# Leaving out nine idle TensorE matmuls of zeros at the start of a gated linear attention and feed-forward kernel

## Chip, cores and metric

The kernel runs on one core of a Trainium2 chip. The metric is the device time of one execution in microseconds (us); lower is better. The median of three timed executions is compared. A separate execution was recorded by the hardware profiler, and every trace row below is from it.

## What is computed

The inputs are q, k, v and alpha of shape (4, 8, 768, 48): batch, heads, sequence and head size. Per batch and head a 48x48 state runs along the sequence, and its output feeds a bilinear feed-forward layer.

```python
def _attn_ref(q, k, v, alpha):
    state = np.zeros((B, H, D, D), dtype=np.float32)
    for t in range(S):
        state = alpha[:, :, t, :, None] * state + np.einsum('bhd,bhe->bhde', k[:, :, t], v[:, :, t])
        y[:, :, t] = np.einsum('bhd,bhde->bhe', q[:, :, t], state)
    return y

x = attn_out.transpose(0, 2, 1, 3).reshape(B * S, H * D)      # 3072 x 384
a = x @ w_a                                                   # 384 x 1536
b = x @ w_b
out = (a * b) @ w_out                                         # 1536 x 384
```

## The kernel before, in words

The work is cut into six chunks. A chunk holds two batches (called `u` 0 and 1) and 256 positions of the sequence, two to a partition. For a chunk the kernel takes the logarithm of alpha, forms running sums of it along the sequence with a triangular matrix on TensorE, and takes exponentials of these sums to scale q and k. Then it transposes the scaled q and k on TensorE or by DMA, forms scores, masks them, multiplies by v and carries the state over to the next chunk. The result, already transposed, goes through the feed-forward layer in units of 128 hidden columns.

The order of all instructions is written by hand in a table of text, `PROGRAM`. Each line names a chunk and then short operations, and the kernel issues them in exactly that order; each engine then works through its own instructions in that order and waits on semaphores for what it needs. The part of the table around the change is the first stage, chunk 0, which has the following steps.

- `ld a`, `ld k`, `ld q` with `Y` (SP's queue) or `P` (POOL's queue) load the inputs; `0a` and `0b` are the two halves of the heads of batch 0, and `1` is all of batch 1. `c1` fills small constants on VectorE, among them `wz`, a 128x512 tile of zeros (L471).
- `ln` takes logarithms on ScalarE into the tile `la` (L554).
- `B` forms running sums, by four fp32 matmuls for one half of the heads (L589 and L590). In chunk 0 there are four such groups: `B 0b`, `B 0a`, `B 1a` and `B 1b`. The profile shows each fp32 matmul as two records, so each group has eight records.
- `E` takes the two exponentials of the sums on ScalarE (L665, into the tile shown as `prod`), and `mk` and `mq` scale k and q with them on VectorE into `QKp` (L676).
- `dk` forms the sums over 64 positions on TensorE by 32 small matmuls (L698), and `de` takes their exponentials on ScalarE into `bl` (L719).
- `C` transposes the eight head pairs of one half of the heads on TensorE, keys first and then queries (L736), and `Ce` copies the result out of PSUM into `kqT` on VectorE (L960).
- `v` and `vs` copy v into its place on ScalarE (L769 and L958).
- `D` forms scores (L837), `K` the new state (L792), `k` scales it into `Sm` (L819), `SB` multiplies the carried state by the queries (L866), `M` masks (L846), `Y` multiplies by v (L866).
- `a` and `b` are the units of the feed-forward layer (L921), `o` its second product (L943).

Two places of the first stage hold an operation `fill n i`: it issues n matmuls of zeros by zeros into PSUM bank i, whose result nothing reads.

```python
    def fill(n, i):
        for _ in range(n):
            nc.tensor.matmul(bank(i), lhsT=wz[:, :C], rhs=wz, start=True, stop=True)

    def cum_both(ch, uh, i):                                   # "B"
        ...
        for r in range(2):
            nc.tensor.matmul(p[:, r], lhsT=ut, rhs=x[:, :, 0, :], start=True, stop=False)
            nc.tensor.matmul(p[:, r], lhsT=ut if r else uts, rhs=x[:, :, 1, :], start=False, stop=True)
```

The seven matmuls of `fill 7 0` are TensorE's first instructions. The two of `fill 2 0` stand between the two groups of transposes of batch 0.

Of the kernel before, what the change touches and what calls it, by code (L numbers as in the profile page):

```python
# [14 lines left out]


PROGRAM = """
0: cm 0; c1; cz 0 b P; ci; ld a 0b Y; c1a; ld a 0a Y; ln 0b; cu; cz 1 b P; fill 7 0; cu2 V
0: cz 0 q V; cus; ld k 0b Y; ld k 0a Y; B 0b 2; ld q 0b Y; ln 0a; B 0a 0; ld v 0 P; ld q 0a Y; ld a 1 P; cs 0 m P
0: E 0b i; mk 0b V; ld k 1 P; ld q 1 P; cm 1; W b 0 256; cz 0 v P; E 0b b; mq 0b V; ld v 1 P; W a 256 768; dk 0 2  # L20
0: C 0 1 3; E 0a i; mk 0a V; cz 1 q P; E 0a b; mq 0a V; v 0 S; Ce 0 1 V; fill 2 0; W a 0 256; de 0; W b 256 512
0: C 0 0 1; Ce 0 0 V; D 0 1 2; K 0 0 0; vs 0 0 S; W b 512 768; cs 1 m P
1: ld a 0 P
0: D 0 0 4; k 0 0 V; SB 0 0; M 0 0; ln 1; B 1a 6
# [1153 lines left out]
```

## Time and profile before

| what | value |
|---|---|
| median of three timed executions | 189.08 us (189.05 to 189.28) |
| time of the profiled execution | 190.44 us |
| its span, first to last instruction | 188.7 us |
| TensorE (PE) busy | 181.9 us, 96% of the span |
| VectorE (DVE) busy | 152.6 us, 81% |
| ScalarE (ACT) busy | 120.1 us, 64% |
| GpSimd (POOL) busy | 53.6 us, 28% |
| mean granted TensorE clock | 0.991 of full speed |

The profiled execution is 1.74 us longer than its span, the part before the first and after the last instruction. PE is the matmul side of TensorE and PEld its weight loads. Times of rows are counted from the start of the span. In a row of the timeline stand the start, the length of the merged instructions, engine, source line, operation, output and inputs, shape, the count, and in brackets the idle time of the engine just before with what released it. Matmuls are pipelined and the records of neighbours overlap, so a busy PE is not one at its peak. In a row of a table by stretches, the fields are the length of the stretch, each engine's busy time with its count of instructions, the granted TensorE clock (PEclk), the busy share of DMA and its GB/s.

### The profile page before, as it was taken

The numbers are of one execution on the slowest core, as the hardware profiler recorded it, in microseconds if no ns is written. First come the engines' busy times: TensorE is split into PE (matmuls) and PEld (weight loads), VectorE is DVE, ScalarE is ACT, GpSimd is POOL, SyncE is SP. The second block draws the span as 40 slices with busy tenths as digits, with TensorE's granted clock in tenths as the row PEclk, the third lists the DMA queues.
The fourth block names the chain that finished last, engine by engine and source line by source line (L and its number), as shares of the span: only waits on it lengthen the run. The fifth ranks groups of instructions, "written<-read, shape, count | busy, mean of one in ns | idle before, by whom it ended". The sixth has DMA issues, their size and how long they took to land.

```text
span 188.7 us, 6347 instructions
## 1 busy us (share of the span) xinstructions
PE 181.9 (96%) x2693; PEld 122.3 (65%) x2709; DVE 152.6 (81%) x271; ACT 120.1 (64%) x228; POOL 53.6 (28%) x74
## 2 busy tenths in 40 slices
PE   7979999999999999999999999999999999999993
PEld 3969886566778886754445644555457477565992
DVE  2484889788979799998889899999999945696862
ACT  4364865579995797797697949965980451526230
POOL 8999654998062240003500003300000000000000
PEclk9987999999999999999999999999999999999999
DMA  5999999999999899989999699939500102110053
GB/s 125 263 225 195 261 235 254 230 231 257 247 214 129 129 215 276 275 237 182 198 173 271 144 116 167 112 107 165 89 0 9 43 0 83 44 43 0 0 170 127
DMA packets 66285, 29.43 MB, mean 156 GB/s; under 512 B 55776, under 2 KB 64624, under 8 KB 66256
## 3 DMA queue, kind: packets, MB, share of 16 engines
q1 hardware_dynamic: 47488, 16.34, 41.2%
q0 software_dynamic: 18624, 12.58, 39.3%
q8 instruction: 21, 0.34, 0.7%
q10 hardware_dynamic: 144, 0.10, 0.2%
q14 instruction: 8, 0.07, 0.1%
HBM read 25.98 MB, written 4.74 MB: 163 GB/s over the span
## 4 chain that ended last, share of the span: by engine, by line
PE 90%; ACT 6%; issue 2%; DVE 1%
PE psum L921 47%; PE psum L943 12%; PE psum L1032 11%; PE psum L866 5%; PE psum L837 3%; PE psum L589 2%; PE psum L590 2%; PE psum L736 2%; PE psum L572 2%; ACT vx L958 2%; PE psum L631 1%; ACT la L554 1%; PE psum L792 1%; PE psum L805 1%; PE psum L698 1%
## 5 line engine op out<-in xcount | busy, mean ns | idle before, releaser
L921 PE MATMUL psum<-xT,wb_t 128*128 128x512 bf16 (+1 forms) x263 | 55.8, 336 | 0.5 <-issue 0.2
L921 PE MATMUL psum<-xT,wa_t 128*128 128x512 bf16 (+1 forms) x262 | 55.2, 335 | 0.5 <-issue 0.2
L921 PEld LDWEIGHTS <-wa_t 128*128 128x128 bf16 x270 | 25.7, 98 | 19.2 <-issue 0.5
L921 PEld LDWEIGHTS <-wb_t 128*128 128x128 bf16 x270 | 25.5, 98 | 18.4 <-issue 0.5
L943 PE MATMUL psum<-wo_t,prod 128*128 128x384 bf16 x144 | 26.1, 327 | 0.0
L958 ACT ACTIVATE ot<-psum 128x384 f32<-128x384 f32 (+1 forms) x23 | 11.2, 487 | 17.7 <-PE psum L1032 15.4
L650 POOL TENSOR_TENSOR q_t<-q_t,ra 128x384 f32<-128x384 f32 x6 | 6.4, 1072 | 53.6 <-ACT ra L643 31.1
L943 PEld LDWEIGHTS <-prod 128*128 128x128 bf16 x144 | 13.3, 98 | 8.3
L958 ACT ACTIVATE vx<-v_t 32x384 bf16<-32x384 bf16 x26 | 13.5, 521 | 1.5 <-DVE vx L771 1.1
L1032 PEld LDWEIGHTS <-prod 128*128 128x128 bf16 x144 | 12.0, 98 | 1.2
L850 ACT ACTIVATE m<-psum 128x768 bf16<-128x768 f32 x14 | 11.0, 810 | 2.3 <-PE psum L837 2.3
L676 DVE TENSOR_TENSOR QKp<-q_t,beta 128x768 bf16<-128x768 f32 x10 | 9.4, 952 | 1.9 <-ACT beta L665 1.6
L554 ACT ACTIVATE la<-a_t 128x1536 f32<-128x1536 f32 (+2 forms) x9 | 9.5, 1054 | 1.7 <-DMA a_t<-in_alpha_dram 1.5
L676 DVE TENSOR_TENSOR QKp<-k_t,invb 128x768 bf16<-128x768 f32 x10 | 10.1, 1013 | 0.3
L846 DVE TENSOR_TENSOR m<-psum,mask 128x768 bf16<-128x768 f32 x10 | 9.5, 949 | 0.6 <-PE psum L837 0.6
L1044 DVE TENSOR_TENSOR ot<-psum,ot 128x384 f32<-128x384 f32 x9 | 5.0, 555 | 5.9 <-issue 3.2
L866 PE MATMUL psum<-m,vx 64*64 64x128 bf16 (+1 forms) x576 | 8.7, 205 | 0.0
L547 POOL DMA_DIRECT2D v_t<-in_v_dram x8 | 8.5, 1064 | 0.0
L866 PE MATMUL psum<-kqT,Sm 64*64 64x128 bf16 x144 | 7.5, 220 | 0.4 <-DVE Sm L819 0.4
L866 PEld LDWEIGHTS <-vx 64*64 64x64 bf16 x576 | 7.6, 108 | 0.1
L854 DVE TENSOR_TENSOR m<-m,mask 128x768 bf16<-128x768 bf16 x14 | 7.4, 550 | 0.0
L665 ACT ACTIVATE prod<-psum 128x384 f32<-128x384 f32 x8 | 3.5, 488 | 6.0 <-PE psum L590 6.0
(292 smaller groups left out, 361.5 us busy)
## 6 DMA issues: line engine op xcount, KB each, us to landing
out_dram<-ot SPq DMA_DIRECT2D x23, 192.0 KB, 2.7
q_t<-in_q_dram SPq DMA_DIRECT2D x3, 768.0 KB
k_t<-in_k_dram SPq DMA_DIRECT2D x3, 768.0 KB
a_t<-in_alpha_dram POOLq DMA_DIRECT2D x2, 768.0 KB, 11.7
v_t<-in_v_dram POOLq DMA_DIRECT2D x4, 384.0 KB, 7.6
a_t<-in_alpha_dram SPq DMA_DIRECT2D x2, 768.0 KB
a_t<-in_alpha_dram POOLq DMA_DIRECT2D x3, 384.0 KB, 7.5
k_t<-in_k_dram POOLq DMA_DIRECT2D x3, 384.0 KB, 7.3
```

Source lines behind the costliest of these rows:

```text
L547: eng.dma_start(out=t[:, us, hs].rearrange("p b h r d -> p (b h) (r d)"), in_=src[ch.b0 + us.start:ch.b0 + us.stop, hs, ch.s * 2 * C:(ch.s ...
L554: nc.scalar.activation(out=ch.la[:, us, hs].rearrange("p b h r d -> p (b h r d)"), in_=ch.a[:, us, hs].rearrange("p b h r d -> p (b h r d) ...
L650: eng.tensor_mul(x, x, by)
L676: eng.tensor_mul(QKp[ch.c % 2][:, u, j, :, hs, :D], src[:, u, hs].rearrange("p h r d -> p r h d"), f)
L846: nc.vector.tensor_mul(m, x, maskn())
L850: nc.scalar.activation(out=m, in_=x, func=AF.Copy)
L854: eng.tensor_mul(m, m, maskn())
L866: nc.tensor.matmul(o, lhsT=lhsT, rhs=rhs, start=(g, c) not in begun, stop=False, skip_group_check=True)
L921: nc.tensor.matmul(p, lhsT=(wa_t, wb_t)[w][:, kk, f * 128:(f + 1) * 128], rhs=ch.xT[:, kk, us, :], start=(kk == 0), stop=(kk == KT - 1))
L943: nc.tensor.matmul(op, lhsT=ch.prod[:, f, at:at + C], rhs=wo_t[:, f, :], start=(f == 0), stop=(f == NFF - 1))
L958: nc.scalar.activation(out=o_, in_=i_, func=AF.Copy)
L1032: nc.tensor.matmul(o[:, g], lhsT=A[:, f, g * C:(g + 1) * C], rhs=W[:, f], start=(not more and (apart or g == 0) and f == 0), stop=(f == LH ...
```

## The change

Both `fill` operations are taken out of the table. Everything else stays: the tile of zeros is still filled, and no instruction of another engine moves.

```diff
-0: cm 0; c1; cz 0 b P; ci; ld a 0b Y; c1a; ld a 0a Y; ln 0b; cu; cz 1 b P; fill 7 0; cu2 V
+0: cm 0; c1; cz 0 b P; ci; ld a 0b Y; c1a; ld a 0a Y; ln 0b; cu; cz 1 b P; cu2 V
...
-0: C 0 1 3; E 0a i; mk 0a V; cz 1 q P; E 0a b; mq 0a V; v 0 S; Ce 0 1 V; fill 2 0; W a 0 256; de 0; W b 256 512
+0: C 0 1 3; E 0a i; mk 0a V; cz 1 q P; E 0a b; mq 0a V; v 0 S; Ce 0 1 V; W a 0 256; de 0; W b 256 512
```

On PE, at the head of the program, these are the last of the seven zero matmuls and the first running sums of `B 0b` before the change (`la` is the logarithm, `ut` and `uts` are the triangular matrices, and the waits name the engine whose semaphore is waited for).

```order
L572 LDWEIGHTS wz
L572 MATMUL psum<-wz 128x512
L589 MATMUL psum<-la,ut 128x192 [waits DVE_49,Activation_49]
L590 MATMUL psum<-la,uts 128x192 [waits DVE_49]
L589 MATMUL psum<-la,ut 128x192
```

After the change the running sums follow the program's entry directly.

```order
L1173 UNCONDITIONAL_BRANCH [waits barrier_Pool_Activation_PE_DVE_SP_release]
L589 MATMUL psum<-la,ut 128x192 [waits DVE_49,Activation_49]
L590 MATMUL psum<-la,uts 128x192 [waits DVE_49]
L589 MATMUL psum<-la,ut 128x192
```

The wait of the first running sum for ScalarE's logarithm is the same in both; only what PE does ahead of it is gone.

The second place on PE is between the last transpose of one half of the heads of batch 0 and the first of the other half (`QKp` holds the scaled q and k, `ident` is the identity).

```order
 L736 MATMUL psum<-ident,QKp_85 128x128
-L572 LDWEIGHTS wz
-L572 MATMUL psum<-wz 128x512 [waits Activation_49]
-L572 LDWEIGHTS wz
-L572 MATMUL psum<-wz 128x512
+L736 LDWEIGHTS QKp_85 [waits DVE_49]
+L736 MATMUL psum<-ident,QKp_85 128x4x32 [waits Activation_49]
```

The wait for ScalarE, which has to have read PSUM bank 0, moves from the zero matmul to the first transpose behind it.

## Prediction

> **What bounds the kernel now.** I read the page first, for the engine that carries the span.
>
> ```profile
> PE 181.9 (96%) x2693; PEld 122.3 (65%) x2709; DVE 152.6 (81%) x271; ACT 120.1 (64%) x228; POOL 53.6 (28%) x74
> PEclk9987999999999999999999999999999999999999
> ```
>
> PE is busy for 96% of the span, and the granted clock dips only in slices 3 and 4, from about 9 to 19 us. Next come the waits of PE from 24 us to 185 us.
>
> ```profile
> PE psum L921 <- issue: 0.3, 2, 0.2
> ```
>
> PE waits for nothing there but 0.3 us. So PE's queue after the first stage is solid: whatever the first stage loses or gains by the time PE enters it should arrive at the end nearly whole. The question is when PE leaves the fp32 running sums of `B 1b` at about 17 us. For this I read PE's timeline; a bracket shows idle time.
>
> ```profile
> 1.19 3.17 PE L572 MATMUL psum<-wz 128*128 128x512 bf16 x7 [1.19 <-DVE og L472]
> 4.15 0.99 PE L589 MATMUL psum<-la,ut 128*128 128x192 f32 x2
> ...
> 7.79 0.91 PE L698 MATMUL psum<-og,la 128*48 128x2 f32 x32
> ...
> 9.08 0.38 PE L572 MATMUL psum<-wz 128*128 128x512 bf16 x1
> 9.51 0.61 PE L736 MATMUL psum<-ident,QKp 128*128 128x128 bf16 x8
> 10.58 0.34 PE L837 MATMUL psum<-kqT 64*64 64x128 bf16 x13 [0.46 <-ACT bl L719]
> ...
> 11.80 0.35 PE L866 MATMUL psum<-kqT,Sm 64*64 64x128 bf16 x6 [0.43 <-DVE Sm L819]
> 12.53 0.85 PE L589 MATMUL psum<-la,ut 128*128 128x192 f32 x2 [0.37 <-ACT la L554]
> ```
>
> The zero matmuls end just as the logarithm arrives, so they delay little. Their work must be looked for in the clock. The chain of waits gives the length of one running-sum matmul at different moments (two records make one matmul).
>
> ```profile
> 5.14 0.64 PE psum L590 x2
> 5.78 0.45 PE psum L589 x2
> 6.23 0.33 PE psum L590 x2
> ...
> 7.53 0.34 PE psum L590 x2
> 7.87 0.02 issue
> ...
> 14.67 0.64 PE psum L590 x2
> ...
> 16.75 0.33 PE psum L590 x2
> ```
>
> The same matmul takes 0.64 us or 0.33 us: half clock or full clock. It changes inside the piece at 5.78, and again shortly after 16. The table by stretches dates the later changes.
>
> ```profile
> 12.00:14.00 2.00, 1.63 (x11) 1.47 (x6) 1.94 (x4) 0.48 (x1) 2.00 (x4) 0.68 1.43 187
> 14.00:16.00 2.00, 2.00 (x8) 2.00 (x7) 0.18 (x2) 0.66 (x2) 2.00 (x4) 0.50 1.51 195
> 16.00:18.00 2.00, 2.00 (x50) 1.76 (x53) 1.25 (x3) 1.10 (x4) 1.95 (x4) 0.97 1.36 192
> ```
>
> A mean of 0.68 over 12 to 14 means that the clock fell to 0.50 at 12.0 + (2 x 0.68 - 1) x 2 = 12.72, and 0.97 over 16 to 18 that it rose at 16.12. They are 3.40 us apart. Two such steps before 12.72 is 5.92, inside the piece that shows the first rise. So the clock is decided at steps of 3.40 us: 5.9, 9.3, 12.7, 16.1. Cut there, the table shows what precedes each decision; the first figure after the length is PE's busy time.
>
> ```profile
> 0.00:2.50 2.50, 1.31 (x4) 0.49 (x5) 0.40 (x4) 1.28 (x1) 1.70 (x12) 1.00 0.18 34
> 2.50:5.90 3.40, 3.40 (x11) 2.17 (x10) 0.91 (x4) 1.05 (x2) 3.33 (x7) 1.00 1.01 246
> 9.30:12.70 3.40, 2.08 (x64) 1.68 (x64) 2.85 (x6) 2.97 (x6) 3.35 (x6) 1.00 1.05 243
> 12.70:16.10 3.40, 3.40 (x12) 3.40 (x13) 1.55 (x4) 0.76 (x2) 3.40 (x6) 0.50 1.54 190
> ```
>
> (The 1.00 before 5.9 is only the absence of a record; the lengths 0.64 show half clock.) A full stretch, 3.40 of 3.40, is followed by full clock, at 5.9 and at 16.1. The stretch with 2.08 of 3.40, 61%, in small matmuls and transposes, is followed by half clock. The first 2.50 us, with 1.31 busy, did not raise it.
>
> **The change part by part.** *The seven matmuls at the head.* Without them PE starts at 4.15, when the logarithm is there. The zero matmuls may have held it up by at most 0.2 us (the chain counts them to 1.19 + 3.17 = 4.36); at half clock that gain is small and I take 0. The stretch 2.50 to 5.90 is then busy for 5.90 - 4.15 = 1.75 us, 51%. Of the rows above, 2.08 busy lost the clock and 3.40 gained it; 51% lies nearer the former, so I take it that the clock stays at half until 9.3. All eight running-sum matmuls of batch 0 then take 0.64: 4.15 + 8 x 0.64 = 9.27, with the 0.17 us by which a last matmul's record outlasts its spacing 9.44, against 7.87 before: 1.57 us later. From 9.3 on PE has the full clock, because 5.90 to 9.30 is all busy.
>
> What hides this? ScalarE's rows:
>
> ```profile
> 7.89 0.87 ACT L665 ACTIVATE prod<-psum 128x384 f32<-128x384 f32 x2 [0.43 <-PE psum L590]
> 9.44 0.84 ACT L769 ACTIVATE vx<-v_t 128x768 bf16<-128x768 bf16 x1 [0.68 <-DMA v_t<-in_v_dram]
> 10.19 0.34 ACT L719 ACTIVATE bl<-psum 48x8 f32<-48x8 f32 x2
> 10.55 1.06 ACT L958 ACTIVATE vx<-v_t 32x384 bf16<-32x384 bf16 x2
> 11.63 0.84 ACT L554 ACTIVATE la<-a_t 128x768 f32<-128x768 f32 x1
> ```
>
> Its exponentials start 1.57 later, at 9.46, and end at 10.33. It waited 0.68 us for v before; that slack goes, so its copy of v starts at 10.34, 0.90 later, and `bl` at 11.09, the `vx` copies and the logarithm of batch 1 follow 0.90 later, so that `B 1a` starts at 13.43 instead of 12.53.
>
> PE and VectorE in between must not be later than that:
>
> ```profile
> 8.89 0.59 DVE L676 TENSOR_TENSOR QKp<-q_t,prod 128x384 bf16<-128x384 f32 x1
> 9.41 1.44 DVE L960 COPY kqT<-psum 128x1024 bf16<-128x1024 bf16 x2
> 11.30 0.36 DVE L819 TENSOR_TENSOR Sm<-psum,bl 128x192 bf16<-128x192 f32 x1 [0.45 <-PE psum L792]
> ```
>
> The last product is 1.57 later, 10.46 to 11.05; the two copies run to 10.97 + 1.44 = 12.41, `Sm` to about 12.8 and PE's six matmuls on it (0.35) to 13.3. This is inside 13.43 by 0.1 us, so ScalarE's logarithm is what ends last.
>
> *Batch 1's sums.* Here the clock repays. Before, from 12.53: 0.2 us at full clock are 0.6 matmuls, 3.40 us at half clock 5.3, the other 2.1 take 0.69, end 16.82. After, from 13.43, with the clock still falling at 12.7 and rising at 16.1: 2.70 us at half clock are 4.2 matmuls, the other 3.8 take 1.25, end 17.38. The difference is 0.56 us.
>
> *The two matmuls among the transposes.* At full clock they lie between 9.08 and 9.51; but the query transposes behind them need the product that ends at 8.89 + 0.59 = 9.48, and the copies of `kqT` start at 9.41 with the other half. So they cost nothing now and leaving them out gives 0 (bounds: their 0.43 us as a gain; and, should their activity be what holds the clock, a loss inside the cases below).
>
> *Sum.* +0.56 us on the profiled execution's 190.44, that is 191.0. The timed runs lie 1.36 below the profiled execution; I carry the difference over to their median: 189.08 + 0.56 = 189.6.
>
> **The rivals.** A measurement of this kernel can tell about 0.2% from no change, 0.38 us.
>
> *Faster: the clock does not fall at 12.7.* The stretch before it is now fuller: the 0.91 us of `dk` and the transposes move into it, and the idle times of 0.46, 0.43 and 0.37 shrink, to about 0.75 us in all, so some 78% busy against 61%. If that holds the clock, `B 1a` and `B 1b` take 8 x 0.33 from 13.43 and end at 16.07, 0.75 before 16.82: 188.3. Against it: most of this is small work, as in the stretch that lost the clock. The Trainium skill, "TensorE: Matmul & The Clock Gate", section "Why this matters for your kernels", says that only gaps of more than about 3 us between bursts bring the half clock back; by it the clock holds here, which is this rival. The trace disagrees, since the clock fell after gaps of at most 0.46 us. Chance 0.20.
>
> *Slower by more: the clock falls at 12.7 and doesn't rise at 16.1.* The stretch 12.7 to 16.1 begins with 0.73 idle and is 78% busy, which lies between the rows of 61% and 100%. Then all eight matmuls are at half clock, 13.43 + 5.12 = 18.55, and what follows until 19.5 also suffers, by 0 to 0.5: +1.73 to +2.2, 190.8 to 191.3, middle 191.0. Chance 0.18.
>
> *No change: 51% is enough at 5.9.* All of it is full-width fp32 work, unlike the small matmuls of 9.3 to 12.7. Then every row behind 5.9 is as before: 189.1. Chance 0.12.
>
> *The decisions fall elsewhere in the timed runs.* All of the above takes the profiled execution's 5.9, 9.3 and so on. The Trainium skill, again "TensorE: Matmul & The Clock Gate", section "Part 1: The HAM clock gate (the "warmup" mystery)", says that the window runs freely and that one kernel showed 6, 11 or 14 slow matmuls. No run here shows a second position; the three times within 0.23 us speak for one position, because half against full clock is worth 8 x 0.31 = 2.5 us in each group of eight sums. Bounds: -1.7 (5.3 half-clock matmuls of batch 1 saved) to +1.8 (2.5 less the 0.68 that ScalarE hides). Chance 0.15.
>
> **How the numbers follow.** My forecast, the cold first sums with half of the delay repaid, has 0.35. It is +0.56 with some 0.3 either way, as the margins of 0.1 and 0.2 us go, so 0.06 of it falls within 0.38. Faster: 0.20 and 0.04 of the last case, 0.24. Within: 0.06, 0.12 and 0.04, 0.22. Slower: 0.29, 0.18 and 0.07, 0.54. The range goes from 188.2, which holds the faster rival, to 191.1, the middle of the slow one and a little more; outside lie about half of the slow rival and the ends of the last case.
>
> **What would show it.** In the changed profile the eight first sums at L589 and L590 should all be spaced 0.64 apart and `dk` (L698) start near 9.35 instead of 7.79; ScalarE's 0.68 us wait for v should be gone, and `la` of batch 1 start near 12.5. PEclk should be 0.50 from 12.7 to 16.1. `dk` of batch 1 should start near 17.6 instead of 17.01. I am wrong if the sums turn fast at 5.9, if no stretch at 0.50 follows 12.7, if half clock lasts beyond 16.1, or if PE shows new waits between 24 and 185 us that swallow the delay.

## The result and the profile after

The changed kernel takes 189.72 us in the median of 22 executions (188.96 to 191.33), the kernel before 189.06 us in 22 executions beside it (188.41 to 190.75). The ratio is 1.0041, with a 95% interval of 1.0022 to 1.0059: slower by 0.66 us between the medians. Ratios here and below leave out executions more than 1.5% above the fastest of their kernel, while the medians hold all of them. The forecast was 189.6. The number came true; the working behind it largely did not, as the profile shows at once. The profiled execution took 190.53 us, 0.81 above the median, and its span is 188.7 us, the same as in the profile of before.

The page's busy times and its row of the granted clock:

```profile
PE 178.6 (95%) x2685; PEld 120.5 (64%) x2700; DVE 152.0 (81%) x271; ACT 120.2 (64%) x228; POOL 51.9 (27%) x74
PEclk9999999999999999999999999999999999999999
```

The dip to half clock that the profile of before has between 12.7 and 16.1 us is not there. PE's timeline of the first stage (start, length, engine, line, operation):

```profile
4.11 1.01 PE L589 MATMUL psum<-la,ut 128*128 128x192 f32 x2 [4.11 <-ACT la L554]
...
6.83 0.84 PE L589 MATMUL psum<-la,ut 128*128 128x192 f32 x2
7.47 0.52 PE L590 MATMUL psum<-la,uts 128*128 128x192 f32 x2
7.83 0.49 PE L589 MATMUL psum<-la,ut 128*128 128x192 f32 x2
...
8.57 0.91 PE L698 MATMUL psum<-og,la 128*48 128x2 f32 x32
...
12.52 0.59 PE L589 MATMUL psum<-la,ut 128*128 128x192 f32 x2
...
15.32 0.91 PE L698 MATMUL psum<-og,la 128*48 128x2 f32 x32
...
19.21 0.83 PE L921 MATMUL psum<-xT,wa_t 128*128 128x256 bf16 x6 [0.16 <-DMA wa_t<-in_moe_w_a_dram]
```

The first sums follow one another at 0.64 us until 7.47 and at 0.33 us from 7.83: the clock rose at about 7.5, not at 5.9 and not at 9.3. It then held, the sums of batch 1 ran at 0.33 us, and PE reached the feed-forward units (L921) at 19.21, where the profile of before has 20.68. So this execution was 1.47 us ahead at that point, and ended with the same span. Against the same matmuls of the profile of before, the lead is 0.84 us at 24.61, 0.39 at 105.55 and gone at 149.74, where this execution is 0.09 behind. At each loss stands a wait of PE; here are its waits from 17 to 185 us (engine, what waits, releaser: us in total, times, longest):

```profile
PE psum L866 <- issue: 0.8, 2, 0.5
PE psum L921 <- issue: 0.3, 2, 0.2
PE psum L866 <- DVE m L846: 0.3, 1, 0.3
PE psum L921 <- DMA wa_t<-in_moe_w_a_dram: 0.2, 1, 0.2
```

The 0.8 us on "issue" are two pauses of PE inside the products with v, for which the profile shows no releaser. The 0.3 on the mask `m` is the third place, at 137.42; the two waits on "issue" at L921 stand in the profile of before as well. The timeline shows the two pauses.

```profile
23.84 0.59 PE L866 MATMUL psum<-m,vx 64*64 64x128 bf16 x37 [0.52 <-issue]
...
104.47 0.34 PE L866 MATMUL psum<-m,vx 64*64 64x128 bf16 x12 [0.25 <-issue]
```

ScalarE's rows show the slack of the prediction used up, and nothing beyond it lost:

```profile
8.68 0.87 ACT L665 ACTIVATE prod<-psum 128x384 f32<-128x384 f32 x2 [0.73 <-PE psum L590]
9.44 0.84 ACT L769 ACTIVATE vx<-v_t 128x768 bf16<-128x768 bf16 x1
11.62 0.85 ACT L554 ACTIVATE la<-a_t 128x768 f32<-128x768 f32 x1
```

The exponentials are 0.79 us later than before, the copy of v starts at 9.44 as before, without its wait of 0.68 us, and the logarithm of batch 1 is where it was.

### The profile page after: what moved, and what is told of

It reads as the page before. It is cut to its first block, busy times and chain, and to the rows that moved or that the text cites. A ratio compares the mean times of both kernels' runs of the same rounds, so it can differ in the third digit from the quotient of the medians.

```text
span 188.7 us, 6330 instructions
## 1 busy us (share of the span) xinstructions
PE 178.6 (95%) x2685; PEld 120.5 (64%) x2700; DVE 152.0 (81%) x271; ACT 120.2 (64%) x228; POOL 51.9 (27%) x74
## 4 chain that ended last, share of the span: by engine, by line
PE 79%; DMA 5%; POOL 5%; ACT 4%; issue 3%; DVE 1%; SPq 0%; POOLq 0%
PE psum L921 44%; PE psum L943 12%; PE psum L1032 11%; PE psum L866 5%; DMA wa_t<-in_moe_w_a_dram 4%; PE psum L837 2%; DMA bl<-row 1%; PE psum L631 1%; ACT vx L958 1%; PE psum L805 1%; POOL v_t L547 1%; PE psum L736 1%; ACT la L554 1%; PE psum L792 1%; POOL mask L503 1%
## 5 line engine op out<-in xcount | busy, mean ns | idle before, releaser
L921 PE MATMUL psum<-xT,wb_t 128*128 128x512 bf16 (+1 forms) x263 | 55.8, 336 | 0.5 <-issue 0.2
L921 PE MATMUL psum<-xT,wa_t 128*128 128x512 bf16 (+1 forms) x262 | 55.2, 335 | 0.7 <-issue 0.2
L921 PEld LDWEIGHTS <-wa_t 128*128 128x128 bf16 x270 | 25.7, 98 | 19.4 <-issue 0.5
L921 PEld LDWEIGHTS <-wb_t 128*128 128x128 bf16 x270 | 25.6, 98 | 18.3 <-issue 0.3
L676 DVE TENSOR_TENSOR QKp<-q_t,beta 128x768 bf16<-128x768 f32 x10 | 9.5, 954 | 1.9 <-ACT beta L665 1.6
L676 DVE TENSOR_TENSOR QKp<-k_t,invb 128x768 bf16<-128x768 f32 x10 | 9.6, 955 | 0.3
L866 PE MATMUL psum<-m,vx 64*64 64x128 bf16 (+1 forms) x576 | 9.0, 205 | 0.8 <-issue 0.8
L589 PE MATMUL psum<-la,ut 128*128 128x192 f32 x16 | 5.2, 417 | 4.2 <-ACT la L554 4.1
L866 PEld LDWEIGHTS <-vx 64*64 64x64 bf16 x576 | 7.7, 108 | 1.2 <-issue 1.0
L866 PE MATMUL psum<-kqT,Sm 64*64 64x128 bf16 x144 | 7.5, 220 | 0.6 <-DVE m L846 0.3
```

The source lines that it names most:

```text
L676: eng.tensor_mul(QKp[ch.c % 2][:, u, j, :, hs, :D], src[:, u, hs].rearrange("p h r d -> p r h d"), f)
L866: nc.tensor.matmul(o, lhsT=lhsT, rhs=rhs, start=(g, c) not in begun, stop=False, skip_group_check=True)
L921: nc.tensor.matmul(p, lhsT=(wa_t, wb_t)[w][:, kk, f * 128:(f + 1) * 128], rhs=ch.xT[:, kk, us, :], start=(kk == 0), stop=(kk == KT - 1))
```

## The experiments

Below, an execution is also told by its mean granted clock, because a fall of the clock for one stretch of 3.41 us lowers that mean to 0.991 (3.41 x 0.5 / 188.7 = 0.009), and two stretches to about 0.98. The late first rise does not lower it, since the record of the clock begins with that rise. All ran beside the kernel before.

**Both kernels once more.** The kernel before:

> The kernel before, unchanged, for a second profile. Clock theory: the decisions of the clock stand elsewhere than in the first profile; where none falls into the idle stretch of 10 to 12.5 us, the clock doesn't fall, TensorE starts the feed-forward units near 19.1 instead of 20.7 us, and the span is 1 to 1.6 us under 188.7. Rival (the position is fixed): fall at 12.7 again, span 188.7. In time: within 0.3 us of before, since it is the same kernel.

The changed kernel:

> The changed kernel, unchanged, for a second profile. Stream theory (pauses come where TensorE's instruction stream has a multiple of 256, and the change moves these places by 18 instructions into the products with v): the pauses stand again at the same instructions, at record counts near 705 and 3264, at whatever clock. Rival (they were chance): none there. In time: 0.5 to 1.2 us above before.

The kernel before took 189.07 us (12 executions), ratio to itself 0.9986 (0.996 to 1.0012); its span is 187.0. The changed kernel took 189.49, ratio 1.0025 (0.9999 to 1.005); its span is 187.2. Their PE timelines, before first:

```profile
6.80 0.59 PE L589 MATMUL psum<-la,ut 128*128 128x192 f32 x2
7.22 0.49 PE L590 MATMUL psum<-la,uts 128*128 128x192 f32 x2
...
12.28 0.59 PE L589 MATMUL psum<-la,ut 128*128 128x192 f32 x2
...
18.74 0.83 PE L921 MATMUL psum<-xT,wa_t 128*128 128x256 bf16 x6
```

```profile
7.46 0.85 PE L590 MATMUL psum<-la,uts 128*128 128x192 f32 x2
8.10 0.56 PE L589 MATMUL psum<-la,ut 128*128 128x192 f32 x2
8.50 0.49 PE L590 MATMUL psum<-la,ut 128*128 128x192 f32 x2
...
12.86 0.59 PE L589 MATMUL psum<-la,ut 128*128 128x192 f32 x2
...
19.32 0.83 PE L921 MATMUL psum<-xT,wa_t 128*128 128x256 bf16 x6
```

The clock now rises at about 7.0 before and 8.2 after, and falls in neither: the position of the decisions is another one in each profile. By the Trainium skill, "TensorE: Matmul & The Clock Gate", section "Part 1: The HAM clock gate (the "warmup" mystery)", the window runs freely; these traces agree. The first profile of before, with its fall, was an exception: of 111 further executions of the kernel before whose clock was recorded, 11 show a mean of 0.991, in the median 191.07 us, and 100 show 0.997 or more, in the median 189.10. So a fall goes with about 2 us, and the time of the kernel before is that of executions without it.

Like against like, the later rise puts the changed kernel 0.58 us behind at 19.32 against 18.74, and 0.28 us of that are left at PE's last products (182.87 against 182.59). The pauses of the first changed profile are absent here: the changed instruction places alone do not make them. The interval of the second comparison holds no change; the loss is clear of noise in the first one, of 22 executions.

A reason why the clock does not fall in the changed kernel stands in the two stretches of 3.41 us behind the rise in its first profile:

```profile
7.53:10.94 3.41, 3.17 (x59) 2.59 (x61) 2.89 (x6) 2.64 (x8) 3.29 (x6) 1.00 1.19 280
10.94:14.35 3.41, 3.10 (x65) 2.73 (x66) 3.16 (x6) 1.72 (x4) 3.41 (x6) 1.00 1.43 207
```

PE is busy for 3.17 and 3.10 us of them, where the stretch that lost the clock before had 2.08 of 3.40. With the later rise, batch 0's small work and waits are shared out between two stretches, and each holds fp32 sums beside them.

**The head alone (called e1_no_head below).** Only the seven matmuls are left out:

```diff
-cz 1 b P; fill 7 0; cu2 V
+cz 1 b P; cu2 V
```

> Only the seven zero matmuls at the head are left out; the two among the transposes stay. Clock theory (the head's activity raises the clock early, which the first sums need): this is where the loss is, so the median is 0.5 to 0.9 us above before, like the full change. Rival (the two in the middle keep the clock up at the next decision): within 0.3 us of before. In the profile: the first sums at 0.64 us each until a decision between about 6.7 and 10.

190.56 us, ratio 1.006 (1.0034 to 1.0086), no execution with a fall. The head's absence is enough for a loss, and a larger one than the whole change. PE's timeline:

```profile
8.04 0.84 PE L589 MATMUL psum<-la,ut 128*128 128x192 f32 x2
8.69 0.53 PE L590 MATMUL psum<-la,ut 128*128 128x192 f32 x2
...
10.44 0.59 PE L572 MATMUL psum<-wz 128*128 128x512 bf16 x2
10.87 0.61 PE L736 MATMUL psum<-ident,QKp 128*128 128x128 bf16 x8
```

The clock rises at about 8.7. The middle matmuls are followed at once by the transposes at 10.87. As before the change, these could not have ended much earlier: the scaled queries are ready at 10.25 + 0.55 = 10.80 (L676). So this stretch does not show why the kernel loses more than the full change; PE's pauses, which are longer in its profile (two of 0.51 and 0.48 us), are a candidate.

**The middle alone (e2_no_mid).** Only the two matmuls are left out:

```diff
-Ce 0 1 V; fill 2 0; W a 0 256
+Ce 0 1 V; W a 0 256
```

> Only the two zero matmuls among batch 0's transposes are left out. Clock theory with the head as cause: within 0.3 us of before. Rival (the middle two matter): 0.4 to 0.9 us above before. In the profile: the first sums as in before, the transposes of the other half of the heads up to 0.3 us earlier.

190.15 us, ratio 1.0018 (0.9979 to 1.0057), which holds no change, for a reason: the times fall into groups. Six executions with a mean clock of 0.998 or more take 188.80 us in the median, three with 0.991 take 190.41, three near 0.98 take 191.63.

**The same instruction places with little activity.** The matmuls stay and write 2 columns, first all nine (e3_tiny), then the head's seven (e5_head_tiny), then the middle two (e6_mid_tiny):

```diff
-            nc.tensor.matmul(bank(i), lhsT=wz[:, :C], rhs=wz, start=True, stop=True)
+            nc.tensor.matmul(bank(i)[:, :2], lhsT=wz[:, :C], rhs=wz[:, :2], start=True, stop=True)
```

> All nine zero matmuls stay, but each writes 2 columns instead of 512, so the instruction stream has the same length and the same places and hardly any activity. Clock theory: as slow as the full change, 0.5 to 0.9 us above before. Rival (the change moves all later TensorE instructions by 18 places, and the pauses of 0.52 and 0.25 us that the changed profile shows inside the products with v at 23.3 and 104.2 us come from that): within 0.3 us of before, and no such pauses in the profile.

> The seven zero matmuls at the head write 2 columns instead of 512, the two in the middle stay as they are: the clock of e1_no_head, the instruction places of before. Stream theory: no pauses of 0.5 us at counts 705 and 3264, so some 0.8 to 1.0 us below e1_no_head's 1.35 above before, that is 0.3 to 0.6 above before. Clock theory alone: like e1_no_head, 1.0 to 1.4 above before.

> The two zero matmuls in the middle write 2 columns instead of 512, the seven at the head stay: the instruction places of before, less activity ahead of the idle stretch. Clock theory: more executions in which the clock falls in or behind the idle stretch, so a second group of times 1.2 to 1.6 us above the fastest, as in e2_no_mid (7 of 12 at 190 or more). Stream theory: e2_no_mid's slow group came from its places, moved by 4; with them restored, within 0.3 us of before and no more slow runs than before has.

All nine small: 189.82, which is 0.61 above the 189.21 of the kernel before beside it, as expected for the clock, but the ratio of 1.0017 (0.999 to 1.0044) holds no change; no falls, where 6 of the 35 executions beside it fell. The head's seven small: 190.31, ratio 1.0056 (1.003 to 1.0082), no falls. The middle two small: 190.75, ratio 1.0071 (1.0039 to 1.0102), falls in 11 of 12 executions: seven with 0.991 (190.63), four near 0.98 (191.74), and one without (188.75). So restoring the places does not restore the time where the result is clear of noise, and each kernel goes with its counterpart that leaves the matmuls out: late rise and no falls without the head's activity, many falls without the middle's. The theory that the shift by 18 instructions is the cause falls, and with it the reading of the slow groups without the middle two as ones of places. Here is a fall in the table by stretches (length, PE's busy time first, PEclk third from the end), for the kernel with the middle two small:

```profile
9.17:12.58 3.41, 2.21 (x65) 1.70 (x63) 3.03 (x6) 2.87 (x6) 3.37 (x6) 1.00 1.07 244
12.58:15.99 3.41, 3.41 (x13) 3.41 (x12) 2.03 (x5) 0.87 (x2) 3.41 (x6) 0.50 1.53 188
```

**More zero matmuls in the idle time.** Six more, on top of the nine:

```diff
-C 0 0 1; Ce 0 0 V; D 0 1 2;
+C 0 0 1; fill 2 6; Ce 0 0 V; D 0 1 2;
...
-D 0 0 4; k 0 0 V; SB 0 0; M 0 0; ln 1; B 1a 6
+D 0 0 4; k 0 0 V; fill 2 6; SB 0 0; M 0 0; ln 1; fill 2 6; B 1a 6
```

> The kernel before with six more zero matmuls, two in each of TensorE's three idle times between 10 and 12.5 us (ahead of the scores, ahead of the carried-state product and ahead of batch 1's sums). Clock theory: the clock no longer falls at 12.7, the sums of batch 1 take 0.33 us each and TensorE reaches the feed-forward units up to 1.5 us earlier, limited by the weights that land at about 19.2; if that lead reaches the end, 0.8 to 1.5 us below before. Rival (the lead is lost later to transfers and pauses, as in the changed profile, where a lead of 1.7 us at 17 us had become a lag of 0.1 at the end): within 0.3 us of before although the clock holds.

190.43 us, ratio 1.0055 (1.0026 to 1.0083). No execution fell, and both theories missed. Against the second profile of before, PE starts batch 1's sums 0.37 us later (12.65), is 0.45 behind at 24.04, still 0.25 at 134.13, and 1.00 at 136.91, after a wait for a mask on VectorE; why most executions are slower still than the profiled one (189.74) stays open.

**How many.** Four at the head instead of seven (`fill 4 0`), and four in the middle instead of two (`fill 4 0` there):

> Four instead of seven zero matmuls at the head (about 1.2 to 2.9 us, then 1.2 us of idle time before the first sums), the two in the middle as before. Clock theory (a stretch of about 3.4 us must be nearly all busy for the clock to rise): four do little, the rise comes as late as without a head in most executions (6.7 to 10 us), the median is 0.9 to 1.4 above before as in e1_no_head and e5_head_tiny, and no execution shows a fall (mean clock 0.991). Rival (the rise comes with the amount of activity): a median 0.2 to 0.6 above before, and some falls.

> Four instead of two zero matmuls among the transposes, the seven at the head as before. If the middle matmuls are what keeps the clock from falling in the idle stretch of 10 to 12.5 us: executions with a mean clock of 0.991 or less go from 10 of 82 to none of 12; against that stand 0.43 us more of zero matmuls in the path, so the median is 0.1 to 0.5 above before. Rival (what counts is only where the decision falls): 1 or 2 of 12 fall as before, the same cost.

Four at the head: 190.94 (6 executions), ratio 1.0092 (1.0061 to 1.0123), no falls; in the profile the clock rises at about 8.4. They did nothing that none would not do, against the rival by which the amount counts. It fits that a stretch has to be nearly full, since here 1.06 us are idle before the first sum; one profile and six executions are all there is for it. Four in the middle: 189.34, ratio 0.9996 (0.9975 to 1.0018), no falls in 12; the ratio does not show the cost that was expected.

**The middle's activity at another place.** The two are taken from among the transposes, and one (e9_later_one), then two, put at each of two later waits:

```diff
-Ce 0 1 V; fill 2 0; W a 0 256
+Ce 0 1 V; W a 0 256
...
-D 0 0 4; k 0 0 V; SB 0 0; M 0 0; ln 1; B 1a 6
+D 0 0 4; k 0 0 V; fill 1 6; SB 0 0; M 0 0; ln 1; fill 1 6; B 1a 6
```

> The head's seven stay, the two in the middle move into the later waits of the idle stretch: one ahead of the carried-state product, one ahead of batch 1's sums. If the activity in the stretch decides the fall, wherever it stands in it: falls as in before (0 to 3 of 12) and a median of executions at full clock near e2_no_mid's 188.8, so 0 to 0.3 us below before. Rival (it must stand among the transposes): falls as in e2_no_mid and e6_mid_tiny, 6 to 11 of 12, and a median 0.9 to 1.5 above before.

> As e9_later_one with two zero matmuls at each of the two places. No falls (0 or 1 of 12); the four matmuls take 0.86 us, of which some 0.4 us lie in waits, so the executions at full clock are 0.2 to 0.5 us slower than e9_later_one's. Rival: falls in half or more of the executions, median 0.9 or more above before.

One at each place: falls in 6 of 12, 188.83 without and 190.64 with one; median 189.45, ratio 1.0029 (0.9998 to 1.0059). The falls are as many as the rival expected, so two matmuls at these places keep the clock less well than among the transposes; the median is below the rival's 0.9. Two at each: no falls, 189.23, ratio 0.9997 (0.9979 to 1.0015). Neither this nor the four in the middle beats the kernel before by more than the measurement can tell. Together they show no fall in 24 executions; at before's 11 in 111 two or three would be expected, so that they end the falls altogether is not shown.

## Why the prediction came true, point by point

The forecast was met with luck. By its own signs the working failed: no stretch at half clock follows 12.7 in the changed profile, and PE shows new waits between 24 and 185 us. Its +0.56 starts from a delay of 1.57 us, where 0.62 and 0.79 were measured, and takes off a repayment by the clock that does not take place.

| zero matmuls: head, middle | executions that fell | median of those that did not, us |
|---|---|---|
| 7, 2 (before) | 11 of 111 | 189.10 |
| 0, 0 (after, twice) | 0 of 34 | 189.72 and 189.49 |
| 0, 2 and 4, 2 | 0 of 18 | 190.56 and 190.94 |
| 7, 0 | 6 of 12 | 188.80 |
| 7, 2 small | 11 of 12 | 188.75 (one) |
| 7, 1+1 later | 6 of 12 | 188.83 |
| 7, 4 and 7, 2+2 later | 0 of 24 | 189.34 and 189.23 |

*The zero matmuls act through the clock: right.* Without a full head the rise comes late, at 7.4 to 8.8 us in all six profiles of such kernels; with it, at 4.3 to 7.0 us in all eight. With small matmuls in the same places the head does nothing.

*"51% ... I take it that the clock stays at half until 9.3": right in direction, wrong in size.* In no profile without a full head did the clock rise before 7.4. But the steps stand elsewhere each time, so the sums end 0.8 to 0.6 us later than before (`dk` at 8.57 and 8.91 against 7.79 and 8.29), not 1.57. The case that the decisions fall elsewhere, to which I gave 0.15, is what holds in nearly every execution; my reason against it, three times within 0.23 us, was too little, since 100 of 111 executions lie between 188.24 and 190.25 us, while the rise moves by up to 2.7 us from one profile with a full head to another.

*ScalarE's slack: right.* In the first changed profile it hid all of a delay of 0.79 us; in the second pair ScalarE has no slack in before (its copy of v starts at 9.19 without a wait), and the logarithm of batch 1 moves by 0.58, from 11.38 to 11.96.

*The fall at 12.7 and the half repaid: wrong.* None of 76 executions without a full-size head of seven fell after the rise. The delay is not repaid in clock, because the typical execution of before doesn't fall either. I took a single profile for the typical one; its mean clock of 0.991 against 0.997 or more in 100 of 111 says that its 1.36 us over the median went with the fall, and carrying them over hid this.

*The two in the middle at 0: wrong.* With the head and without them, 17 of 24 executions fall, at 1.6 to 1.9 us for one fall, while the seven that don't fall have medians 0.3 us below before's. Without the head there is no fall to keep off, and there they cost: 190.56 and 190.31 with them, 189.5 to 189.8 without or small. By the medians the full change is then milder than either half of it, though the ratio of the kernel without the middle two alone is not clear of noise. Leaving out the head makes the middle two needless; why they cost some 0.8 us there, when the two take 0.43, stays open. PE's pauses, told of below, take 1.0, 0.7 and 1.2 us in the three profiles with a middle and no full head, and 0.8, 0 and 0.2 in the three without either, which is a hint and no proof.

*Nearly whole to the end: only in part.* Of 0.58 us at the entry of the feed-forward units 0.28 were left in the second pair. In the first changed profile, against the second of before, the lag grows instead: 0.47 us at 19.21, 1.02 at 24.61, behind the pause at 23.84, 1.27 at 105.55, behind that at 104.47, and 1.80 at 151.03, behind the wait for a mask at 137.42; the spans differ by 1.7. The prediction had no such pauses. So, as far as two pairs of profiles tell, the 0.66 us are a late rise that costs 0.2 to 0.6, and pauses on top in some executions; how many pause was not recorded. That 0.56 came near it was luck.

## What to carry to other kernels

Look at the mean clock of many executions before taking one profile's stretch at half clock for the kernel's usual course: here it was one execution in ten. Warming matmuls are judged as a whole: the head brought an early rise, and with it the risk of a fall, which the middle two made rare; by the medians each alone was worse than none. Let a warm-up reach right up to the work it serves: here four matmuls with an idle microsecond behind them were worth nothing.

## What was not expected of the hardware

Inside the small products at L866, PE paused without a releaser in five of the six profiles of kernels without a full head, for 0.2 to 0.5 us at a time, and in none of the eight with one. (The 0.16 us before two units at L921 are found in both kinds.) For four matmuls at the head:

```profile
17.72 0.30 PE L866 MATMUL psum<-kqT,Sm 64*64 64x128 bf16 x4 [0.37 <-issue]
...
24.46 0.66 PE L866 MATMUL psum<-m,vx 64*64 64x64 bf16 x43 [0.46 <-issue]
```

Counted in the records on PE's queue (matmuls, weight loads and three of the program's entry), 448 or 449, 704 or 705, and 3261 to 3266 of them stand ahead of a pause, whatever the kernel has at that count. These are 256 and 10 x 256 apart, within the few records that a trace lacks, and each pause ends 2.3 to 2.8 us after one of the 16 KB packets on the queue for instructions has started. But where there is no pause, the record at a count of 705 starts 2.5 to 2.8 us after such a packet too, so this time does not tell the two apart. That PE waits there for its own instructions is argued and not shown, and why only kernels with a late rise do so stays open. A fall, too, does not follow from PE's busy time alone: stretches of 2.08 and 2.21 us busy of 3.4 lost the clock, while one of 2.11 kept it in the profile with one matmul at each of the later waits, and one of 2.23 in that with two. And it came after idle times of at most 0.46 us, so the rule of the Trainium skill, "TensorE: Matmul & The Clock Gate", section "Why this matters for your kernels", that drops are avoided by leaving no idle gap of more than about 3 us, does not suffice here.
